# Batch 1 of a Fourier-mixing and GEGLU kernel loaded and folded like batch 0, with the weights ahead of it in the DMA queue

## The chip, the cores and the metric

One core of one Trainium2 chip. The metric is the device time of a run in microseconds (us); the time of before is the median of three runs. The core has a matrix engine (TensorE, PE), which takes a weight tile (LDWEIGHTS) and streams columns past it (MATMUL) into PSUM; a vector engine (VectorE, DVE); an activation engine (ScalarE, ACT); a general engine (GpSimd, POOL); and a sequencer (SyncE, SP) that here issues nearly all DMA transfers. Each engine works through its own instructions in the order in which the program gives them.

## The reference

`x` has 8 batches of 3008 tokens with 256 features. Each batch gets the real part of a two-dimensional Fourier transform (over tokens and features), and then every token goes through a gated feed-forward block with 1536 hidden units:

```python
X = np.fft.fft(x, axis=1)
X = np.fft.fft(X, axis=2)
x = X.real.astype(np.float32).reshape(B * S, D)

g = x @ w_gate
gelu = 0.5 * g * (1.0 + erf(g * inv_sqrt2))
val = x @ w_val
return (gelu * val @ w_out).astype(np.float32)
```

## The kernel before

**The transform.** 3008 = 64 x 47. A token index is split into 64 values on the partitions and 47 columns j. The kernel uses the symmetry of the real transform: feature f and feature 256 - f are added and subtracted first (the "folds"), so that 128 even and 128 odd values are left of 256. Stage one is a transform of length 64 along the partitions by tables of sines and cosines, stage two one of length 47 (`b_steps`, tables `TPQ`). Only 1505 of 3008 output rows are made (`Y`); the mirrored ones come from the even and odd parts of the layers that follow. The feature transform itself is folded into the weights: `gen_w` multiplies `w_gate` and `w_val` by a 256-point cosine table (`CW`) and leaves them as `WE`, `WOP`, `WOM`.

**Two ways through stage one.** Batch 0: `load_x` brings each third of the columns as three DMAs straight from `x`, with the partner columns (47 - j) on the odd partitions and the far columns in slots 4 to 7 of an `xin` buffer. `singles_first` and `fold_first` make 24 columns of folded data in `xf`, and `a_group` multiplies them by the table `G` (24 columns of 128). Batches 1 to 7: the tokens that are needed in mirrored order of the 64 are first copied, turned, from HBM to HBM (`flip`, two DMAs per batch, tile `xr`), and `load_x` takes four DMAs per third, two from `x` and two from `xr`. Then both folds are done (`fold_part`, two column pairs at a time, even step k = 0 and 2, odd step k = 1 and 3), which leaves 12 columns, and `a_step` multiplies each by a 128 x 128 table `GA` (made from `G` by `gen_ga`), two columns of 256 per step. Its result goes to HBM (`z_write`, tile `z`) and comes back with other partitions (`z_read`, into `Ap`) for stage two. POOL does the folds, but for batch 1 the step (1, 0) of `DVE_FOLDS` is DVE's.

**The layers.** The work is cut into units: batch, one of three chunks of rows, one of 12 tiles of 128 hidden units; 36 units a batch, 288 in all, numbered u, with i = u mod 36. In each unit PE does layer one (matmuls of up to 512 columns for gate and value, even, odd plus, odd minus), ACT the Gelu, DVE and POOL the products into `h`, and PE some matmuls of layer two of the chunk before (`Wo_sb`, 256 columns each) by the counts in `STEPS`. In the units of `SPLIT` the minus gate isn't a matmul of its own but is put together by ACT, DVE and POOL (`ge`, `go`).

**The order** is written out by hand. Ahead of the units stand batch 0's transform and the loads of the weights, in pieces of 256, 256, 512 and 512 columns; POOL casts them to bf16 (`cast_w`), and `gen_w` runs ahead of the units and in units 0 to 7 (`extra`): the last 512 columns in units 4 to 7. `f_units`, `a_units` and `r_units` say in which units the folds, `a_step`s and `z_read`s of the next batches stand; `plan` gives the units of stage two (from 22 on in batch 0). Layer two begins at the end of unit 12.

```python
    for f0, n in ((256, 256), (512, 512)):
        for i in (1, 0):
            load_w(f0, i, n)
    flip(1)
    pool.memset(xins[0][:, 4, :], 0.0)
    for i in (1, 0):
        load_w(1024, i)
    for i in range(3):
        load_x(1, i)
```

Of the kernel before, what the change touches and what calls it, by code (L numbers as in the profile page):

```python
# [10 lines left out]
BF16 = mybir.dt.bfloat16  # L11
INT32 = mybir.dt.int32
AF = mybir.ActivationFunctionType
ALU = mybir.AluOpType
# [24 lines left out]
def kernel(  # L39
# [24 lines left out]
    B, T, C = x.shape  # L64
# [2 lines left out]
    NJ = 48  # L67
    HJ = 24
    HP = HJ // 2
    DVE_FOLDS = ((1, 0),)  # L70
    KP = 96
    NG = 32
    NCH = C // 128
# [8 lines left out]
    psum = ctx.enter_context(tc.tile_pool(name="psum", bufs=1, space=bass.MemoryType.PSUM))  # L82
    dram = ctx.enter_context(tc.tile_pool(name="dram", bufs=1, space=bass.MemoryType.DRAM))

    G = const_pool.tile([128, HJ, 128], BF16)
    GA = const_pool.tile([128, HP, 128], BF16)
    GH = NG // 2
    TS = 2 * N2
# [120 lines left out]

    xr = {}  # L210

    def flip(b):
        xr[b] = xr_tile()
        for s, (j0, n) in enumerate(((N2 - HP + 1, HP - 1), (HP, HP))):
            d = xr[b][s, :, :, :]
            sync.dma_start(
                out=ap_replace(d, ap=[[C, n], [HP * C, N1], [1, C]], offset=d.offset),
                in_=ap_replace(x, ap=[[C, n], [-N2 * C, N1], [1, C]],
                               offset=x.offset + (b * T + N2 * (N1 - 1) + j0) * C))
# [25 lines left out]
    def singles_first(i):  # L245
        pool.tensor_tensor(
            _sub(xf, [[HP * C, 2], [C, 4], [128, 2]], 4 * i * C),
            _sub(xins[i], [[4 * C, 2], [C, 4], [128, 2]], 0),
            _sub(sg, [[0, 2], [0, 4], [1, 2]], 0), op=ALU.mult)

    def fold_first(i, a0, an):
        at = lambda o, k: _sub(xins[i], [[4 * C, 2], [C, an], [k, 127]], a0 * C + o)
        to = lambda o: _sub(xf, [[HP * C, 2], [C, an], [1, 127]], (4 * i + a0) * C + o)
        vec.tensor_tensor(to(1), at(1, 1), at(255, -1), op=ALU.add)
        for h in range(2):
            lo, hi = (_sub(xins[i], [[C, an], [k, 127]], (4 * h + a0) * C + o) for o, k in ((1, 1), (255, -1)))
            vec.tensor_tensor(
                _sub(xf, [[C, an], [1, 127]], (HP * h + 4 * i + a0) * C + 129),
                hi if h else lo, lo if h else hi, op=ALU.subtract)

    def fold_part(b, i, k):
        eng = vec if b == 1 and (i, k) in DVE_FOLDS else pool
        a0 = k // 2 * 2
        o0 = (HP * (b % 2) + 4 * i + a0) * C
        at = lambda s, o, pat: _sub(xins[i], [[C, 2]] + pat, (s + a0) * C + o)
        if k % 2 == 0:
            eng.tensor_tensor(
                _sub(xf, [[C, 2], [128, 2]], o0), at(0, 0, [[128, 2]]), at(4, 0, [[128, 2]]), op=ALU.add)
            eng.tensor_tensor(
                at(0, 1, [[128, 2], [1, 127]]), at(0, 1, [[128, 2], [1, 127]]),  # L270
                at(4, 255, [[-128, 2], [-1, 127]]), op=ALU.add)
        else:
            for o, op in ((1, ALU.add), (129, ALU.subtract)):
                eng.tensor_tensor(
                    _sub(xf, [[C, 2], [1, 127]], o0 + o), at(0, 1, [[1, 127]]),
                    at(0, 255, [[-1, 127]]), op=op)

# [121 lines left out]

    def sin_g(i):  # L400
        for h in range(2):
            act.activation(
                _sub(G, [[128, 8], [1, 64]], i * 8 * 128 + h * 64),
                _sub(reds[i], [[64, 8], [1, 64]], 0), AF.Sin, scale=col_h[h][:, :], bias=col_o[h][:, :])

    def turn_g(odd):
        nb = 2 if odd else 1
        for to, of, n, sign in (((1, 33, 8, 1.0), (33, 1, 8, -1.0), (3, 35, 8, -1.0), (35, 3, 8, 1.0))
                                if odd else ((0, 0, 16, 1.0), (2, 2, 16, -1.0))):
            pat = [[128, 8], [64, nb], [4, n]]  # L410
            to, of = _sub(G, pat, 16 * 128 + to), _sub(G, pat, of)
            if odd:
                act.activation(to, of, AF.Copy, scale=sign)
            else:
                pool.tensor_scalar(to, of, sign, None, op0=ALU.mult)

    def gen_ga():
        for h in range(2):
            act.activation(
                _sub(GA, [[128, HP], [1, 64]], 64 * h), _sub(G, [[128, HP], [1, 64]], HP * h * 128),  # L420
                AF.Copy, scale=half[:, h : h + 1])

    def phase_t():
# [152 lines left out]
    def a_group(J, v):  # L576
# [5 lines left out]
        for gq in range(2):  # L582
            for e in range(2):
                for jl in range(4):
                    jj = HP * (jl % 2) + 4 * J + 2 * v + jl // 2
                    on_half(ps, pe.matmul(
                        _sub(ps, [[1, 128]], gq * C + e * 128, 32 * jl, 32),
                        _sub(G, [[32, 2], [2, 16]], (jj - 16 * (jj > 15 and gq == 0)) * 128 + 64 * e + gq),
                        _sub(xf, [[1, 128]], jj * C + 128 * e), start=True, stop=True))
        if J:  # L590
            for h in range(2):
# [85 lines left out]
    units = []  # L677
    NU = B * len(CH) * NFC
    PER = NU // B
    STEPS = ((7, 8, 9, 8, 8, 8, 8, 8, 8, 8, 8, 8, 8, 9, 7, 8, 8, 8, 8, 8, 8, 8, 8, 8, 8, 9, 7, 7, 7, 10, 7, 7, 10, 8, 8, 8), (7, 9, 8, 8, 9, 7, 8, 8, 8, 7, 8, 9, 8, 7, 9, 9, 7, 8, 7, 5, 6, 6, 7, 5, 8, 8, 8, 8, 8, 8, 8, 8, 8, 8, 8, 8))  # L680
# [232 lines left out]

    WF = (4, 5)

    def warm(n, w=None):
        ps = ps_d()
        for _ in range(n):
            pe.matmul(ps, G[:, 0, :] if w is None else w, _sub(G, [[1, 512]], 0),
                      start=True, stop=True)  # L920

    for i in (1, 0):
# [81 lines left out]
    for u in range(NU + 2):  # L1004
# [142 lines left out]
```

## Time and profile before

| | |
|---|---|
| median of 3 runs | 619.86 us (619.02 to 620.75) |
| the profiled execution | 617.99 us, of which the span from first to last instruction is 616.0 |
| PE busy | 593.5 us, 96% |
| DVE, POOL, ACT busy | 561.7, 488.0, 473.7 us |
| granted TensorE clock, mean | 0.997 |
| DMA | 79.50 MB, mean 129 GB/s |

A row of the profile names the engine, the operation, what it writes and reads (`xf<-xin`), shapes, a count, and in brackets the idle time before it and what ended that. All instructions pass through one helper, so that nearly every row has line 26 (L26) and rows are told apart by their tiles. `SPq` is SP issuing a DMA; PEld is a weight load. "issue" stands for a wait of which the profile shows no releaser. The duration of one matmul contains its way through the array: matmuls that follow one another start at shorter distances than that.

### The profile page before, as it was taken

The page shows a single profiled execution, that of the slowest core. Times are in us where ns is not written, and L with a number is a line of the kernel's source. Part 1 is how long each engine was busy: PE and PEld are TensorE (multiplying, and loading weights), DVE is VectorE, ACT ScalarE, POOL GpSimd, SP SyncE. Part 2 cuts the span into 40 slices and gives each one's busy share as a digit, 9 for nine tenths or more (in the row PEclk, how much of TensorE's full clock was granted, in tenths as well). Part 3 has the DMA queues.
Part 4 walks back from the last instruction along what each step waited for, and adds up shares of the span by engine and source line. Part 5 has one row for each costly group of instructions (what it writes and reads, how often), then busy time and mean ns, then how long its engine had stood idle before and what let it go on. Part 6 is the DMA issues. An engine that isn't in the chain of part 4 may idle for free.

```text
span 616.0 us, 12455 instructions
## 1 busy us (share of the span) xinstructions
PE 593.5 (96%) x4285; PEld 389.4 (63%) x4285; DVE 561.7 (91%) x693; ACT 473.7 (77%) x985; POOL 488.0 (79%) x444
## 2 busy tenths in 40 slices
PE   4979899999999999999999999999999999999997
PEld 2535566666666666666666666666666666666666
DVE  7848889999999999999999999999999999999992
ACT  7868687878788788877878778887788778777762
POOL 6448989898978889898987979888987855666552
PEclk9989999999999999999999999999999999999999
DMA  7797733554543643545435545437224321222123
GB/s 250 237 315 245 240 125 77 160 162 122 160 123 84 192 150 94 156 118 169 142 89 146 155 112 159 133 86 213 63 61 103 80 59 44 61 51 53 38 49 85
DMA packets 75377, 79.50 MB, mean 129 GB/s; under 512 B 9291, under 2 KB 69515, under 8 KB 74643
## 3 DMA queue, kind: packets, MB, share of 16 engines
q1 hardware_dynamic: 73603, 77.81, 43.7%
q0 software_dynamic: 1552, 0.79, 0.9%
q8 instruction: 33, 0.54, 0.4%
q14 instruction: 29, 0.24, 0.1%
q10 hardware_dynamic: 160, 0.13, 0.1%
HBM read 48.52 MB, written 40.72 MB: 145 GB/s over the span
## 4 chain that ended last, share of the span: by engine, by line
PE 84%; DMA 6%; DVE 3%; SPq 3%; POOL 2%; issue 1%; ACT 1%; ACTq 0%; DVEq 0%; POOLq 0%
PE ps_o L26 36%; PE ps_g L26 26%; PE ps_v L26 18%; PE ps_d L26 4%; SPq L26 3%; DMA xin<-xr 2%; DMA wst<-in_moe_w_gate_dram 1%; DMA xin<-in_x_dram 1%; DMA Ap<-z 1%; DVE h L26 1%; POOL h L26 1%; DVE dv L26 1%; DVE ev L26 1%; DVE xf L26 0%; POOL go L26 0%
## 5 line engine op out<-in xcount | busy, mean ns | idle before, releaser
L26 POOL TENSOR_TENSOR h<-glm,dv 128x1024 bf16<-128x1024 bf16 (+1 forms) x138 | 291.1, 2112 | 82.4 <-DVE dv L26 43.7
L26 PE MATMUL ps_o<-Wo_sb,h 128*128 128x256 bf16 x2124 | 283.7, 273 | 0.0
L26 PEld LDWEIGHTS <-h 128*128 128x128 bf16 x2208 | 212.2, 98 | 70.3 <-issue 0.2
L26 DVE SCALAR_TENSOR_TENSOR ev<-nq,WN,ps_v 128x512 f32<-128x512 bf16 (+1 forms) x276 | 201.6, 734 | 24.2 <-PE ps_v L26 13.8
L26 ACT ACTIVATE glp<-ps_g 128x512 bf16<-128x512 f32 (+1 forms) x288 | 170.1, 591 | 43.2 <-PE ps_g L26 31.7
L26 ACT ACTIVATE glm<-ps_g 128x512 bf16<-128x512 f32 (+1 forms) x245 | 144.7, 591 | 60.0 <-PE ps_g L26 47.4
L26 DVE TENSOR_TENSOR h<-glp,ps_v 128x1024 bf16<-128x1024 bf16 (+2 forms) x150 | 173.0, 1153 | 8.8 <-ACT glp L26 8.0
L26 DVE SCALAR_TENSOR_TENSOR dv<-ev,ps_v 128x1024 f32<-128x1024 f32 (+1 forms) x138 | 164.9, 1195 | 0.0
L26 PE MATMUL ps_v<-Y,WE 128*128 128x512 bf16 (+1 forms) x288 | 108.3, 376 | 0.0
L26 PE MATMUL ps_v<-Y,WOP 128*128 128x512 bf16 (+1 forms) x288 | 108.2, 376 | 0.1
L26 PE MATMUL ps_g<-Y,WOP 128*128 128x512 bf16 (+1 forms) x288 | 108.1, 375 | 0.0
L26 PE MATMUL ps_g<-Y,WE 128*128 128x512 bf16 (+1 forms) x288 | 108.0, 375 | 0.0
L26 PEld LDWEIGHTS <-WOP 128*128 128x128 bf16 x576 | 55.8, 97 | 60.4 <-issue 1.3
L26 PE MATMUL ps_g<-Y,WOM 128*128 128x512 bf16 (+1 forms) x245 | 92.3, 377 | 0.5 <-DVE WOM L26 0.5
L26 PEld LDWEIGHTS <-WE 128*128 128x128 bf16 x576 | 56.3, 98 | 31.0 <-issue 5.1
L26 POOL TENSOR_TENSOR xf<-xin 128x254 bf16<-128x254 f32 (+1 forms) x125 | 68.4, 564 | 4.2 <-PE ps_d L26 3.6
L26 ACT ACTIVATE osb<-ps_o 128x512 f32<-128x512 f32 x92 | 54.2, 589 | 15.4 <-PE ps_o L26 11.5
L26 POOL TENSOR_TENSOR go<-go,ge 128x480 f32<-128x480 f32 (+1 forms) x43 | 53.0, 1232 | 11.9 <-DVE go L26 11.9
L26 POOL TENSOR_TENSOR xin<-xin 128x508 f32<-128x508 f32 x41 | 51.8, 1264 | 0.0
L26 PE MATMUL ps_d<-tab,Ap 96*128 96x94 bf16 (+2 forms) x246 | 43.8, 204 | 3.1 <-issue 2.1
L26 ACT ACTIVATE Y<-ps_d 128x192 bf16<-128x192 f32 (+5 forms) x156 | 38.8, 381 | 0.3 <-PE ps_d L26 0.3
L26 PEld LDWEIGHTS <-Ap 96*128 96x128 bf16 (+1 forms) x289 | 24.6, 96 | 15.2 <-issue 2.6
(132 smaller groups left out, 325.6 us busy)
## 6 DMA issues: line engine op xcount, KB each, us to landing
out_dram<-osb SPq DMA_DIRECT2D x358, 64.0 KB
xin<-in_x_dram SPq DMA_DIRECT2D x47, 256.0 KB
xin<-xr SPq DMA_DIRECT2D x35, 256.0 KB
xr<-in_x_dram SPq DMA_DIRECT2D x7, 768.0 KB
z<-S SPq DMA_DIRECT2D x21, 256.0 KB
Ap<-z SPq DMA_DIRECT2D x21, 256.0 KB
xr<-in_x_dram SPq DMA_DIRECT2D x7, 704.0 KB
nq<-nrow SPq DMA_DIRECT2D x8, 376.2 KB
```

The lines of the kernel that those rows point to most:

```text
L26: return lambda *a, **k: self._tc.keep_in_program_order(call(*a, **k))
```

## The change

Batch 1 goes through `load_x` and the folds the way batch 0 does: three DMAs per third, straight from `x`, no `flip(1)`. `fold_one` does it in steps of two column pairs as `fold_part` did (even steps with `singles_first`, odd steps with two subtractions), and fills all 24 columns of `xf`. Its stage one has no `GA`: for each of 12 columns j, for even and odd features (e), two products are added in PSUM, of columns j and 12 + j with a table each. For that `G` is laid out anew: for each pair (j, j + 12) and e there are 64 columns of one table, 64 zeros and 64 columns of the other, 192 in all, so that a window of 128 at offset 0 or 64 is one table beside zeros. The zeros are a DVE memset; the second pair of Sin calls becomes four; `turn_g(False)` turns the odd tables as well as the even.

The last third of the weights is issued right behind the second. `load_wo` moves from ahead of the units to unit 4, `gen_ga` from unit 8 to 18, and the memset of slot 4 of `xin` 0 from ahead of the units to unit 10. DVE's fold is step (1, 1). The units of folds, `a_step`s and `z_read`s, `STEPS` and `SPLIT` are written anew.

```diff
-    DVE_FOLDS = ((1, 0),)
+    DVE_FOLDS = ((1, 1),)
...
-    G = const_pool.tile([128, HJ, 128], BF16)
+    GS = 192
+    G = const_pool.tile([128, HP, 2, GS], BF16)
...
+    goff = lambda jj, e: (jj % HP * 2 + e) * GS + jj // HP * 128
...
-        if b == 0:
+        if b < 2:
             put_x(i, 1, 4, 4, xb(N2 - HP - j, [[-C, 4]]))
             put_x(i, 1, 1 - o, 3 + o, xb(N2 - 1 + o - j, [[-C, 3 + o]]))
             put_x(i, 0, 0, 8, xb(j, [[HP * C, 2], [C, 4]]))
...
+    def fold_even(i, a0, an, eng):
         at = lambda o, k: _sub(xins[i], [[4 * C, 2], [C, an], [k, 127]], a0 * C + o)
+        eng.tensor_tensor(
+            _sub(xf, [[HP * C, 2], [C, an], [1, 127]], (4 * i + a0) * C + 1),
+            at(1, 1), at(255, -1), op=ALU.add)
+
+    def fold_odd(i, a0, an, eng):
         for h in range(2):
             lo, hi = (_sub(xins[i], [[C, an], [k, 127]], (4 * h + a0) * C + o) for o, k in ((1, 1), (255, -1)))
-            vec.tensor_tensor(
+            eng.tensor_tensor(
                 _sub(xf, [[C, an], [1, 127]], (HP * h + 4 * i + a0) * C + 129),
                 hi if h else lo, lo if h else hi, op=ALU.subtract)
...
+    def fold_one(i, k):
+        eng = vec if (i, k) in DVE_FOLDS else pool
+        if k % 2 == 0:
+            singles_first(i, k, 2)
+            fold_even(i, k, 2, eng)
+        else:
+            fold_odd(i, k - 1, 2, eng)
...
+    vec.memset(_sub(G, [[GS, 2 * HP], [1, 64]], 64), 0.0)
...
         for h in range(2):
-            act.activation(
-                _sub(G, [[128, 8], [1, 64]], i * 8 * 128 + h * 64),
-                _sub(reds[i], [[64, 8], [1, 64]], 0), AF.Sin, scale=col_h[h][:, :], bias=col_o[h][:, :])
+            for j0, n in ((8 * i, 8),) if i == 0 else ((8, 4), (12, 4)):
+                act.activation(
+                    _sub(G, [[2 * GS, n], [1, 64]], goff(j0, h)),
+                    _sub(reds[i], [[64, n], [1, 64]], 64 * (j0 - 8 * i)), AF.Sin,
+                    scale=col_h[h][:, :], bias=col_o[h][:, :])
...
-            pat = [[128, 8], [64, nb], [4, n]]
-            to, of = _sub(G, pat, 16 * 128 + to), _sub(G, pat, of)
+            pat = [[2 * GS, 8], [GS, 2], [4, n]]
+            to, of = _sub(G, pat, goff(16, 0) + to), _sub(G, pat, of)
...
+            j = 2 * k + i
+            if b == 1:
+                for e in range(2):
+                    for h in range(2):
+                        pe.matmul(
+                            ps[:, i * C + 128 * e : i * C + 128 * e + 128],
+                            _sub(G, [[1, 128]], goff(j, e) + 64 * h),
+                            _sub(xf, [[1, 128]], (HP * h + j) * C + 128 * e), start=(h == 0), stop=(h == 1))
+                continue
...
-    SPLIT = ((13, 25), (1, 5, 7, 11, 19, 25, 31), (1, 5, 7, 11, 25, 31), (5, 11))
+    SPLIT = ((31,), (1, 5, 7, 11, 19, 25, 31), (1, 5, 7, 11, 25, 31), (7,))
...
-    flip(1)
-    pool.memset(xins[0][:, 4, :], 0.0)
     for i in (1, 0):
         load_w(1024, i)
...
-    load_wo()
-    extra = {1: [lambda: cast_w(1024)], 0: [lambda: turn_g(False)], 8: [gen_ga], 17: [gen_tf]}
+    extra = {1: [lambda: cast_w(1024)], 0: [lambda: turn_g(False)], 4: [load_wo], 18: [gen_ga], 17: [gen_tf]}
...
-    a_units = ((9, 10, 11, 13, 14, 17), (1, 2, 5, 6, 8, 12))
-    r_units = ((14, 15, 19), (5, 13, 14))
-    f_units = ((1, 2, 4, 5, 6, 7, 8, 9, 10, 12, 13, 14), (15, 18, 21, 23, 25, 26, 29, 30, 31, 32, 33, 35), (3, 8, 12, 13, 20, 21, 23, 26, 27, 29, 33, 35))
+    a_units = ((8, 9, 10, 11, 12, 14), (0, 2, 6, 7, 9, 12))
+    r_units = ((13, 14, 16), (4, 13, 14))
+    f_units = ((1, 2, 3, 4, 5, 6, 7, 8, 9, 10, 11, 13), (17, 19, 21, 22, 24, 25, 26, 29, 30, 31, 33, 34), (4, 10, 11, 16, 18, 19, 22, 26, 27, 28, 32, 35))
...
+            if b == 0 and i == loads[0]:
+                pool.memset(xins[0][:, 4, :], 0.0)
...
-                    fold_part(1, *divmod(f_units[0].index(i), 4))
+                    fold_one(*divmod(f_units[0].index(i), 4))
```

More of the change, by code (lines that the diff above doesn't have):

```diff
@@ L243, in load_x, with singles_first, fold_first @@
         put_x(i, 1, 4, 4, xv(1, j, [[C, 4]]))
-    def singles_first(i):
+    def singles_first(i, a0=0, an=4):
         pool.tensor_tensor(
[L247 to L251, printed above, removed]
+            _sub(xf, [[HP * C, 2], [C, an], [128, 2]], (4 * i + a0) * C),
+            _sub(xins[i], [[4 * C, 2], [C, an], [128, 2]], a0 * C),
+            _sub(sg, [[0, 2], [0, an], [1, 2]], 0), op=ALU.mult)
+    def fold_even(i, a0, an, eng):
         at = lambda o, k: _sub(xins[i], [[4 * C, 2], [C, an], [k, 127]], a0 * C + o)
-        to = lambda o: _sub(xf, [[HP * C, 2], [C, an], [1, 127]], (4 * i + a0) * C + o)
-        vec.tensor_tensor(to(1), at(1, 1), at(255, -1), op=ALU.add)
+        eng.tensor_tensor(
+            _sub(xf, [[HP * C, 2], [C, an], [1, 127]], (4 * i + a0) * C + 1),
+            at(1, 1), at(255, -1), op=ALU.add)
+    def fold_odd(i, a0, an, eng):
         for h in range(2):
             lo, hi = (_sub(xins[i], [[C, an], [k, 127]], (4 * h + a0) * C + o) for o, k in ((1, 1), (255, -1)))
-            vec.tensor_tensor(
+            eng.tensor_tensor(
                 _sub(xf, [[C, an], [1, 127]], (HP * h + 4 * i + a0) * C + 129),
                 hi if h else lo, lo if h else hi, op=ALU.subtract)
+    def fold_first(i, a0, an):
+        fold_even(i, a0, an, vec)
+        fold_odd(i, a0, an, vec)
+    def fold_one(i, k):
[5 more added lines that the diff above has]
+            fold_odd(i, k - 1, 2, eng)
     def fold_part(b, i, k):
-        eng = vec if b == 1 and (i, k) in DVE_FOLDS else pool
         a0 = k // 2 * 2
@@ L266, in fold_part @@
         if k % 2 == 0:
-            eng.tensor_tensor(
+            pool.tensor_tensor(
                 _sub(xf, [[C, 2], [128, 2]], o0), at(0, 0, [[128, 2]]), at(4, 0, [[128, 2]]), op=ALU.add)
-            eng.tensor_tensor(
+            pool.tensor_tensor(
                 at(0, 1, [[128, 2], [1, 127]]), at(0, 1, [[128, 2], [1, 127]]),
@@ L273, in fold_part @@
             for o, op in ((1, ALU.add), (129, ALU.subtract)):
-                eng.tensor_tensor(
+                pool.tensor_tensor(
                     _sub(xf, [[C, 2], [1, 127]], o0 + o), at(0, 1, [[1, 127]]),
@@ L419, in gen_ga @@
             act.activation(
-                _sub(GA, [[128, HP], [1, 64]], 64 * h), _sub(G, [[128, HP], [1, 64]], HP * h * 128),
+                _sub(GA, [[128, HP], [1, 64]], 64 * h), _sub(G, [[2 * GS, HP], [1, 64]], 128 * h),
                 AF.Copy, scale=half[:, h : h + 1])
@@ L587, in a_group @@
                         _sub(ps, [[1, 128]], gq * C + e * 128, 32 * jl, 32),
-                        _sub(G, [[32, 2], [2, 16]], (jj - 16 * (jj > 15 and gq == 0)) * 128 + 64 * e + gq),
+                        _sub(G, [[32, 2], [2, 16]], goff(jj - 16 * (jj > 15 and gq == 0), e) + gq),
                         _sub(xf, [[1, 128]], jj * C + 128 * e), start=True, stop=True))
@@ L679 @@
     PER = NU // B
-    STEPS = ((7, 8, 9, 8, 8, 8, 8, 8, 8, 8, 8, 8, 8, 9, 7, 8, 8, 8, 8, 8, 8, 8, 8, 8, 8, 9, 7, 7, 7, 10, 7, 7, 10, 8, 8, 8), (7, 9, 8, 8, 9, 7, 8, 8, 8, 7, 8, 9, 8, 7, 9, 9, 7, 8, 7, 5, 6, 6, 7, 5, 8, 8, 8, 8, 8, 8, 8, 8, 8, 8, 8, 8))
-    SPLIT = ((13, 25), (1, 5, 7, 11, 19, 25, 31), (1, 5, 7, 11, 25, 31), (5, 11))
+    STEPS = ((7, 9, 8, 8, 8, 8, 8, 8, 8, 8, 8, 8, 8, 9, 7, 9, 7, 8, 8, 8, 8, 8, 8, 8, 8, 9, 7, 8, 8, 8, 8, 6, 10, 8, 8, 8), (7, 9, 8, 8, 9, 7, 8, 8, 8, 7, 8, 9, 7, 8, 9, 8, 7, 9, 7, 5, 6, 6, 7, 5, 8, 8, 8, 8, 8, 8, 9, 8, 7, 9, 8, 7))
+    SPLIT = ((31,), (1, 5, 7, 11, 19, 25, 31), (1, 5, 7, 11, 25, 31), (7,))
     for b in range(B):
@@ L914, with warm @@
     WF = (4, 5)
-    def warm(n, w=None):
+    def warm(n):
         ps = ps_d()
         for _ in range(n):
-            pe.matmul(ps, G[:, 0, :] if w is None else w, _sub(G, [[1, 512]], 0),
+            pe.matmul(ps, _sub(G, [[1, 128]], 0), _sub(G, [[1, 512]], 0),
                       start=True, stop=True)
```

1 line of the change is left out of this document (removed).

## The prediction

> **What bounds the kernel now.** I read the page first, then busy time by stretch, then who TensorE (PE) waited for, then the timeline at each wait.
>
> ```profile
> PE 593.5 (96%) x4285; PEld 389.4 (63%) x4285; DVE 561.7 (91%) x693; ACT 473.7 (77%) x985; POOL 488.0 (79%) x444
> ```
>
> ```profile
> 23.40:32.90 9.50, 9.34 (x46) 3.98 (x45) 7.81 (x19) 8.95 (x22) 4.62 (x6) 1.00 0.92 314
> 32.90:53.90 21.00, 15.57 (x110) 7.47 (x110) 11.49 (x21) 14.17 (x29) 13.95 (x19) 0.92 0.99 266
> 53.90:75.40 21.50, 19.38 (x128) 12.15 (x127) 20.25 (x24) 15.21 (x28) 19.15 (x25) 1.00 0.86 272
> 75.40:120.00 44.60, 44.60 (x330) 30.06 (x331) 39.71 (x47) 36.29 (x82) 40.40 (x38) 1.00 0.42 123
> 120.00:600.00 480.00, 478.94 (x3388) 317.50 (x3386) 460.26 (x525) 377.47 (x776) 392.59 (x313) 1.00 0.39 110
> ```
>
> Each row gives a stretch, its length, then PE, weight loads, DVE, ACT and POOL busy, the granted clock, the DMA share and GB/s. From 75.4 us on PE is never free (44.60 of 44.60, then 478.94 of 480), so there the time is PE's own work, and a microsecond that PE gains earlier reaches the end. What can be gained lies between 32.9 and 75.4, where PE is idle for 5.43 and 2.12 us. There the DMA engines are full (0.99 and 0.86). So the opening is a matter of the order in which bytes arrive.
>
> ```profile
> PE ps_o L26 <- POOL wb L26: 3.2, 1, 3.2
> PE ps_d L26 <- issue: 2.1, 1, 2.1
> PE ps_v L26 <- DVE h L26: 1.8, 1, 1.8
> PE ps_g L26 <- DVE WOM L26: 0.5, 1, 0.5
> ```
>
> These are all of PE's waits in the two stretches (us in total, times, longest), 7.6 us. I take them one by one.
>
> **Stall A, the last third of W.**
>
> ```profile
> 20.86 1.86 SPq L26 DMA_DIRECT2D xr<-in_x_dram  x2
> 22.76 5.20 SPq L26 DMA_DIRECT2D wst<-in_moe_w_val_dram  x1
> 27.85 1.04 POOL L26 CAST wb<-wst 128x1024 bf16<-128x1024 f32 x1 [0.25 <-DMA wst<-in_moe_w_gate_dram]
> 34.98 1.04 POOL L26 CAST wb<-wst 128x1024 bf16<-128x1024 f32 x1 [3.57 <-DMA wst<-in_moe_w_val_dram]
> 36.06 1.01 PE L26 MATMUL ps_o<-wb,CW 128*128 128x512 bf16 x2 [3.19 <-POOL wb L26]
> 37.27 0.61 PE L26 MATMUL ps_v<-Y,WOP 128*128 128x481 bf16 x1
> 37.67 0.61 PE L26 MATMUL ps_g<-Y,WOM 128*128 128x480 bf16 x1
> 35.00:40.00 5.00, 3.94 (x12) 1.52 (x12) 0.27 (x1) 1.77 (x4) 2.05 (x2) 0.66 1.23 286
> ```
>
> SP issues the two turned copies of batch 1 (`flip(1)`: by the code 12 + 11 rows of 64 KB, 1.5 MB) ahead of W's last columns. POOL casts the second third of W at 27.85, and the last third's first half only at 34.98. PE stands 3.19 us, and the clock after it is 0.66 in the 5 us window: 0.34 x 5 = 1.7 us more (the matmuls of 480 columns start 0.40 us apart). The change takes the 1.5 MB away, and W's last 1.05 MB come next. At the 314 GB/s of that stretch they are in 3.3 us after 27.85, so by 31.2.
>
> POOL gets there a little earlier than it must: `load_wo` no longer stands ahead, but `turn_g(False)` is doubled.
>
> ```profile
> 30.11 1.29 POOL L26 TENSOR_SCALAR G<-G 128x128 bf16<-128x128 bf16 x2
> 19.18 1.42 POOL L26 TENSOR_SCALAR tab<-red,cols 128x24 bf16<-128x24 f32 x4 [4.15 <-ACT red L26]
> 28.83 1.24 POOL L26 DMA_DIRECT2D Wo_sb<-in_moe_w_out_dram  x1
> ```
>
> One of 24 elements takes 0.36 us, one of 128 takes 0.65, so one of 256 some 1.0, and the pair 2.0. POOL: cast to 28.9, turn to 30.9, cast of the last third 30.9 to 32.0 and 32.0 to 33.0. PE wants the first at 36.06 - 3.19 = 32.87. The margin is 0.9 us. I count all of A as gained: -3.2 and -1.7.
>
> An idle 3.19 us brought the lower clock here; the idle 2.12 us of stall C, below, did not (1.00 in its stretch).
>
> **Stall B, a fold on DVE.**
>
> ```profile
> 45.87 0.18 DVE L26 TENSOR_TENSOR xf<-xin 128x4 bf16<-128x4 f32 x1 [3.00 <-DMA xin<-xr]
> 45.95 0.68 DVE L26 TENSOR_TENSOR xin<-xin 128x508 f32<-128x508 f32 x1
> 47.26 0.36 PE L26 MATMUL ps_v<-Y,WOM 128*128 128x480 bf16 x1 [1.81 <-DVE h L26]
> ```
>
> DVE serves in order and stands 3.00 us before its fold of batch 1, whose rows come back through the turned copy. The products behind it are late, and PE waits 1.81 and then 0.5. After the change DVE's fold is the odd half of the same third, still in unit 6, two instructions of 254 in place of 4 + 508, so the same work to 0.1 us. Its rows (by the code 1.05 MB per third, straight from x, behind W) land at about 34.2, 37.3 and 40.5 by the same 314 GB/s, a little less for what of the copy had already moved by 27.85. DVE came to this fold at 42.87 (45.87 - 3.00); without stall A's 4.9 us that is 38.0, and the second third is in at 37.3. I take -2.3, and +0.1 for what may stay of it (1 us if the rows come 1.7 later).
>
> **Stall C, the return of batch 1 from HBM.**
>
> ```profile
> 70.57 0.59 SPq L26 DMA_DIRECT2D Ap<-z  x1
> 75.39 0.21 PE L26 MATMUL ps_d<-tab,Ap 96*128 96x94 bf16 x2 [2.12 <-issue]
> ```
>
> PE stands 2.12 us until the last `z_read`, issued in unit 19 and 4.8 us on the way, is in. Now it is issued in unit 16, and stage one of the last two columns runs in unit 14, not 17. That is three units earlier for a reader that stays in unit 22, at about 2 us each (of 288 units some 22 lie ahead of 75.4, the other 266 fill 525 us). -2.1. Late next would be SP: it stops in unit 10 at `load_x(2, 0)` for the second turned copy, as before, and now also for POOL's memset, which is queued behind that unit's folds; behind SP stand the writes of z from unit 11 on. The slack of 6 us covers it; without it the 2.1 are back.
>
> Gains: 3.2 + 1.7 + 2.3 + 2.1 = 9.3 us.
>
> **What is added on PE.**
>
> ```profile
> 604.03 6.71 PE L26 MATMUL ps_g<-Wo_sb,h 128*128 128x256 bf16 x60
> 79.79 0.29 PE L26 MATMUL ps_d<-tab,Ap 96*128 96x94 bf16 x3
> 43.07 1.34 PE L26 MATMUL ps_d<-CW,wb 128*128 128x1 bf16 x48
> L26 PE MATMUL ps_d<-xf,GA 128*128 128x256 bf16 x84 | 16.0, 273 | 0.0
> L26 PE MATMUL ps_d<-tab,Ap 96*128 96x94 bf16 x228 | 43.4, 207 | 3.1 <-issue 2.1 <-DMA Ap<-z 1.0
> ```
>
> Stage one of batch 1 was 12 matmuls of 256 columns and becomes 48 of 128, each with a weight load. Sixty of 256 columns, each with its own weights, take (6.71 - 0.27) / 59 = 0.109 us each. Three of 94 columns take (0.29 - 0.21) / 2 = 0.04 each, so 128 columns 0.055 to 0.057. The 48 of one column, each with 128 columns of weights, take 0.028 each, so the load is not the limit. 48 x 0.057 - 12 x 0.109 = 2.7 - 1.3 = +1.4 us, all on PE.
>
> In the Trainium skill, "TensorE: Matmul & The Clock Gate", section "Back-to-back issue gap", pairs of weight load and matmul of 128 columns come every 81 ns. By it the term would be 48 x 0.081 - 1.3 = 2.6, and the sum 1.2 us more. This trace doesn't bear it out: the row of 94 columns has 0.04 a pair.
>
> Split units go from 2 to 1 in batch 0 and in batch 7: two more gate matmuls of up to 512 columns, 2 x 0.218 (0.218 is twice the 0.109) = +0.4 us on PE, for less on DVE, ACT and POOL, which the bound does not feel.
>
> **The front.**
>
> ```profile
> 0.85 0.27 DVE L26 MEMSET xin<- 128x256 f32 x1 [0.85 <-PEq L1131]
> 5.30 2.91 ACT L26 ACTIVATE G<-dv,col_o,col_h 128x512 bf16<-128x512 int32 x4
> 8.12 1.31 ACT L26 ACTIVATE G<-G 128x128 bf16<-128x128 bf16 x4
> 8.43 2.44 DVE L26 TENSOR_TENSOR xf<-xin 128x1016 bf16<-128x1016 f32 x3 [1.94 <-DMA xin<-in_x_dram]
> ```
>
> The memset of the zero columns is 24 x 64 = 1536 elements on DVE: 0.8 us by bytes of the 256-element row, 1.6 by elements. The second pair of Sin calls becomes four, half as long each, about +0.4 for the two more. The table G is then ready 1.2 to 2.0 us after 9.43 (8.12 + 1.31), at 10.6 to 11.4, if nothing of it is hidden. Stage one of batch 0 wants DVE's first folds too, which begin at 8.43 with the data and end at 10.87. So 0 to 0.6, and I take +0.1; without that cover it is the whole 1.2 to 2.0.
>
> **Wo, the new danger.**
>
> ```profile
> Wo_sb<-in_moe_w_out_dram POOLq DMA_DIRECT2D x1, 768.0 KB, 16.5
> 53.89 0.60 PE L26 MATMUL ps_o<-Wo_sb,h 128*128 128x256 bf16 x4
> L26 POOL TENSOR_TENSOR xin<-xin 128x508 f32<-128x508 f32 x41 | 51.8, 1264 | 0.0
> L26 POOL TENSOR_TENSOR xf<-xin 128x254 bf16<-128x254 f32 x84 | 59.5, 731 | 0.6
> ```
>
> Wo was issued at 28.83, landed 16.5 us later at 45.3, and is first read at 53.89, in unit 12. Now POOL issues it after three folds of batch 1. POOL's folds cost as before (1.26 and some 0.2 for the single columns an even step, 2 x 0.73 an odd one), and the first waits for its rows at 34.2: 35.6, 37.0, 38.4. So Wo is issued near 38.4 (37.5 if the rows come faster). PE reaches unit 12's layer two earlier than before by 3.2 + 1.7 + 2.3 less 0.1, and later by 1.6, since five steps of stage one lie ahead of it (5 x 8 x 0.057, as above) where three did (3 x 2 x 0.109); so at 48.4. Bounds of the landing: 16.5 us after issue again is 54.9; the bytes alone at 314 GB/s give 41. In between, the engines then have the rest of batch 1 (to 40.5), then 0.4 MB of the nq row spread over 128 partitions, 1.5 MB of turned copy, 0.5 MB of batch 2 and Wo's 0.8 MB: 3.2 MB at 272 GB/s end at 52.2 if all end together, and Wo, which shares them, ends ahead of the last, near 50.2. That case is the nearest to the traffic of that time, and I take it: PE stands 1.8 us. Bounds 0 and 6.5 + 1.7 of clock.
>
> **The sum.** -9.3 + 0.1 (B's rest) + 1.4 + 0.4 + 0.1 + 1.8 = -5.5 us. The profiled execution took 617.99 us (span 616.0), so 612.5; the median of the runs is 619.86, 1.9 above it, so I forecast 614.4. The rest of the change (new units for folds, reads and steps of later batches, steps of layer two with the same sums of 288 and 276 a batch, `gen_ga` in unit 18) falls where PE idles 1.06 us in 480: nothing, unless a step comes late.
>
> **The rivals.**
> 1. Wo is in time. The DMA engines idle for a moment while SP waits for the nq row to land, and Wo's bytes use it. Then the 1.8 fall away: 612.6, 612.3 if DVE's fold, the front and the narrow matmuls cost at their low ends, and 611.2 with a microsecond of what the runs of before differ (619.02 to 620.75). For it: Wo alone needs 3 us. Chance 0.25.
> 2. Wo is later, and the change loses: issued at 39.5, a microsecond later than forecast, with 16.5 us on the way as measured, it lands at 56.0. PE stands 7.6 us, and after more than 3.19 us idle the half clock costs 1.7. -7.3 + 9.3 = +2.0: 621.9. A landing after 55.9 makes the change slower, one between 52.1 (3.7 us idle and the clock) and 55.9 no change. For it: 16.5 us is what was measured. Against it: then the end of W, the copy and batch 1 were in front of it. Chance 0.19, of which 0.09 beyond +0.3%.
> 3. The copy is not what kept W back: the last third still lands near 35, A stays, and the narrow matmuls and Wo eat B and C: 618 to 620. Against it: the engines are full to 1.23 in that very window. Chance 0.08.
> 4. Weight loads and short matmuls don't overlap: 0.028 + 0.055 a pair, 48 x 0.083 - 1.3 = 2.7 in place of 1.4: 615.7. Chance 0.05, since pairs of 256 columns run at 0.109, about twice what 128 would take. This is what the 81 ns of the Trainium skill, quoted above, would give.
>
> **How the numbers follow.** The forecast has chance 0.43 and a range of its own of 613.4 to 616.5. A measurement tells 0.3% (1.9 us) from no change. Faster than 618.0: 0.43 + 0.25 + 0.05 + 0.03 of 3, 0.76; within: 0.10 of 2 and 0.05 of 3, 0.15; slower than 621.7: 0.09. The range 611.2 to 619.6 takes in rival 1 to its low end and rival 3, and leaves out 0.15 above (most of 2) and some 0.05 below.
>
> **What would show it.** In the profile after: no wait of PE on `wb` and clock 1.00 from 25 to 45 us (A); DVE's wait for its fold under 0.5 us (B); no wait of PE before the first Ap of batch 1 (C); matmuls of 128 columns on ps_d 0.057 us apart; PE's first read of Wo_sb near 50 us, and a wait before it of about 2 us; PE without gaps from unit 22 on, so that its unit 22 starts about 5 us earlier. I am wrong if PE waits on Wo_sb for 5 us or more, if POOL's folds make stage one late in units 8 to 14, or if gaps appear after 75 us.

## The result, and the profile after

Four executions of the changed kernel took 619.67, 618.87, 609.35 and 609.91 us, beside 619.02 to 620.75 us of before (median 620.28 of four). Its time over that of before is 0.9831 [0.9803, 0.986], about 609.8 us; this ratio is of the two shorter executions, since the comparison leaves out what lies over 1.5% above the fastest. The profile that came with the result is of the 619.67 us execution (span 617.8). The unedited kernel was therefore run again (first experiment) and gave 609.77 to 611.5 and a profile of 609.77 us (span 607.9). So there are two profiles of one program, "long" and "short" below, and comparing them shows more than either against before.

Busy time by stretch, columns as in the prediction; first the short execution, then the long one:

```profile
23.40:32.90 9.50, 9.37 (x47) 4.16 (x46) 7.65 (x18) 9.13 (x22) 6.66 (x8) 1.00 1.04 369
32.90:53.90 21.00, 19.17 (x179) 11.67 (x178) 17.84 (x25) 16.49 (x33) 17.21 (x26) 1.00 0.91 246
53.90:75.40 21.50, 20.82 (x145) 12.98 (x143) 19.49 (x22) 17.22 (x36) 17.68 (x21) 1.00 0.67 205
75.40:120.00 44.60, 44.60 (x327) 30.40 (x325) 42.47 (x51) 36.90 (x78) 41.10 (x36) 1.00 0.44 125
```

```profile
32.90:53.90 21.00, 11.94 (x101) 6.57 (x100) 18.50 (x16) 9.29 (x19) 15.49 (x23) 0.76 0.79 203
53.90:75.40 21.50, 20.82 (x154) 13.29 (x153) 17.25 (x23) 17.01 (x30) 9.63 (x16) 1.00 0.69 205
```

In the short execution PE is busy 19.17 of 21.00 where it was 15.57 before, at clock 1.00 and no longer 0.92. In the long one it is busy 11.94, at clock 0.76. After 53.9 the two agree (20.82 both). What separates them happens between 32.9 and 53.9, but for 0.8 us ahead of unit 0, which starts at 22.84 in the short and at 23.60 in the long one.

PE's waits, all of the short execution's and then the longest of the long one's (total, times, longest; the waits on `prow`, `S` and `xf` lie in batch 0's transform, ahead of 19 us, in both):

```profile
PE ps_o L26 <- POOL prow L26: 6.5, 7, 4.3
PE ps_v L26 <- DVE h L26: 1.8, 1, 1.8
PE ps_v L26 <- POOL xf L26: 1.2, 1, 1.2
PE ps_d L26 <- ACT S L26: 0.8, 1, 0.8
PE ps_g L26 <- ACT glp L26: 0.7, 1, 0.7
PE ps_v L26 <- DVE xf L26: 0.5, 2, 0.3
```

```profile
PE ps_v L26 <- DVE h L26: 9.1, 1, 9.1
```

The waits on `wb` (stall A) and on the last `z_read` (stall C) are gone from both. There is no wait on `Wo_sb` in either. The wait on DVE's `h`, stall B, has stayed: 1.8 us in one and 9.1 in the other. DVE's rows show what DVE does in that time, in the short and then in the long execution (start, duration; the bracket would give idle time before the row, and there is none). The fold is two instructions: one row holds both in the short execution, and the row of the long one is the second alone (the first took 0.98).

```profile
37.30 3.78 DVE L26 TENSOR_TENSOR xf<-xin 128x254 bf16<-128x254 f32 x2
41.01 0.65 DVE L26 TENSOR_TENSOR h<-glp,ps_v 128x481 bf16<-128x481 bf16 x1
```

```profile
38.97 10.13 DVE L26 TENSOR_TENSOR xf<-xin 128x254 bf16<-128x254 f32 x1
49.02 0.65 DVE L26 TENSOR_TENSOR h<-glp,ps_v 128x481 bf16<-128x481 bf16 x1
```

The fold no longer waits for rows. It runs, and is slow. In the long execution one instruction of 254 elements takes 10.13 us; before, one of 508 elements took 0.68. POOL's rows of the long execution beside it:

```profile
37.92 1.26 POOL L26 DMA_DIRECT2D Wo_sb<-in_moe_w_out_dram  x1
39.20 1.32 POOL L26 TENSOR_TENSOR xf<-xin 128x254 bf16<-128x254 f32 x2
...
40.64 1.25 POOL L26 TENSOR_TENSOR xf<-xin 128x508 bf16<-128x508 f32 x1
...
45.86 0.30 POOL L26 MEMSET xin<- 128x256 f32 x1
...
47.56 1.25 POOL L26 TENSOR_TENSOR xf<-xin 128x508 bf16<-128x508 f32 x1
49.73 0.61 POOL L26 COPY hx<-h 128x512 bf16<-128x512 bf16 x1 [0.92 <-DVE h L26]
```

POOL folds without a break from 39.20 to 48.81 (a memset of 0.30 us among the folds), and DVE's instruction, begun at 38.97, ends at 49.10, as POOL runs out of work. The rows that DVE needs were in: POOL's even step of the same two column pairs, the fold of 40.64, read them without a wait, 7 us before DVE was done. Before, POOL's folds of batch 1 follow one another nearly as closely, after one wait ahead of the first of them:

```profile
41.71 0.22 POOL L26 TENSOR_TENSOR xf<-xin 128x4 bf16<-128x4 f32 x1 [3.58 <-PE ps_d L26]
...
44.74 1.25 POOL L26 TENSOR_TENSOR xin<-xin 128x508 f32<-128x508 f32 x1
46.07 3.37 POOL L26 TENSOR_TENSOR xf<-xin 128x254 bf16<-128x254 f32 x5
```

There DVE, kept until 45.87 by its rows, came to the end of one of POOL's folds (45.99) and got through at once; POOL's next fold took 1.15 us where those behind it took 0.72. Whether the gap of 0.08 us between these two folds, which the folds of the change don't have, let it through isn't shown.

### The profile page after: what moved, and what is told of

Read it like the earlier page. It is cut to its first block, busy times and chain, and to the rows that moved or that the text cites. A ratio compares the mean times of both kernels' runs of the same rounds, so it can differ in the third digit from the quotient of the medians.

```text
span 617.8 us, 12524 instructions
## 1 busy us (share of the span) xinstructions
PE 594.0 (96%) x4323; PEld 391.8 (63%) x4323; DVE 572.3 (93%) x692; ACT 473.6 (77%) x985; POOL 486.0 (79%) x442
## 4 chain that ended last, share of the span: by engine, by line
PE 92%; DVE 4%; ACT 1%; DMA 1%; issue 0%; DVEq 0%
PE ps_o L26 38%; PE ps_g L26 29%; PE ps_v L26 20%; PE ps_d L26 6%; DVE xf L26 2%; DVE h L26 1%; DMA xin<-in_x_dram 1%; ACT glm L26 0%; ACT glp L26 0%; DVE ev L26 0%; DVE dv L26 0%; ACT GA L26 0%; DVE WOM L26 0%; ACT S L26 0%; DVE G L26 0%
## 5 line engine op out<-in xcount | busy, mean ns | idle before, releaser
L26 POOL TENSOR_TENSOR xf<-xin 128x254 bf16<-128x254 f32 (+2 forms) x124 | 72.7, 601 | 0.0
L26 POOL TENSOR_TENSOR go<-go,ge 128x480 f32<-128x480 f32 (+1 forms) x41 | 50.5, 1231 | 5.8 <-DVE go L26 5.8
L26 POOL TENSOR_TENSOR xin<-xin 128x508 f32<-128x508 f32 x36 | 45.5, 1264 | 0.0
L26 ACT ACTIVATE S<-ps_d 128x512 bf16<-128x512 f32 (+1 forms) x43 | 25.2, 586 | 10.4 <-PE ps_d L26 10.4
```

Source lines behind the costliest of these rows:

```text
L26: return lambda *a, **k: self._tc.keep_in_program_order(call(*a, **k))
```

## The experiments: what holds DVE's fold

The theory: DVE's fold, which reads two operands from SBUF, is held up while POOL folds without a pause; how long depends on whether it meets POOL's break at `load_wo`. The rivals: the rows of that third are late after all; or Wo's transfer and its place are what makes the long executions. All ratios below are over runs of before beside them, with a 95% interval.

**The change again, unedited.**

> The changed kernel once more, unedited. In its first profile DVE's second fold of batch 1 (128x254) took 10.13 us where 0.4 is usual, POOL was folding without a pause at that time, and PE stood 9.06 us. Theory: where DVE gets through, the fold takes 0.4 us, the kernel takes 608 to 611 us, PE has no wait over 2 us after unit 4, and what it gains over the kernel before is the stalls A, B and C (9 us) less 2 us of matmuls and about 1 us before Wo. Rival: the 10 us are always there and hide gains elsewhere: 618 to 620 in all executions.

610.52 us (609.77 to 611.5, four runs), 0.9848 [0.9828, 0.9869]. Its profile is the short one above. With the first four, 2 executions of 8 were long. The profiles don't bear out the theory's part on `load_wo`. In the short execution the fold begins in that break of POOL (37.30; the break lasts from 36.43 to 37.69), but its two instructions end behind it, at 39.53 and 41.09, between folds of POOL. In the long one the first ends in the break (39.04; the break ends at 39.18), and the second is the one held for 10.13 us.

**All folds on POOL.**

```diff
-    DVE_FOLDS = ((1, 1),)
+    DVE_FOLDS = ()
```

> The changed kernel with all folds of batch 1 on POOL, none on DVE. Theory (DVE's fold reads two operands from the same memory as POOL's folds and is held off while POOL reads without a pause): no DVE instruction over 1.5 us between 30 and 60 us, PE's 9 us wait is gone in every execution; POOL is 1.3 us later with what follows, so 609 to 612 us. Rival (the long DVE instruction has to do with the stretch, with DMA or with the clock, and not with the two engines): another DVE instruction between 35 and 50 us takes several us, and about half of the executions stay at 618 to 620.

611.65 us (609.57 to 615.16), 0.9881 [0.985, 0.9912]. The wait on `h` is gone, and the next one shows:

```profile
PE ps_o L26 <- DMA Wo_sb<-in_moe_w_out_dram: 1.0, 1, 1.0
```

So B's wait was DVE's fold, but it was hiding one on Wo: without it PE comes to layer two before Wo (issued at 37.41, 12.2 us on the way) is in. Two of six runs took 615 us; neither of these was profiled, and their cause is open.

**Wo ahead of the units again.** POOL's break of 1.26 us at `load_wo` moves away from the fold; Wo itself comes earlier.

```diff
+    load_wo()
-    extra = {..., 4: [load_wo], 18: [gen_ga], ...}
+    extra = {..., 18: [gen_ga], ...}
```

> The changed kernel with load_wo back ahead of the units, as in the kernel before. Theory by the forecast's term (PE stands 1.8 us for Wo in unit 12): 1 to 2 us faster than the changed kernel, as long as W's last third and batch 1 still come in time, though Wo's 0.8 MB then delay them by some 2 us. Rival (Wo is in time in unit 4 as well, and early it only takes bytes from batch 1): 0 to 3 us slower. In its profile the wait of PE on the third of W or on DVE's fold shows which.

617.95 us (609.35 to 620.24, twelve runs, ten of them above 615), 0.9943 [0.9914, 0.9971]. Neither expected range held (1 to 2 us faster, 0 to 3 slower): an earlier Wo made the kernel 7.4 us slower than the change, so Wo's transfer isn't what the long executions wait for. The profile has the fold and the wait:

```profile
37.24 9.06 DVE L26 TENSOR_TENSOR xf<-xin 128x254 bf16<-128x254 f32 x1
```

```profile
PE ps_v L26 <- DVE h L26: 7.4, 1, 7.4
```

Here the first of the two instructions is held. It ends at 46.30, 0.28 us after the last of POOL's train (46.02), and the second, beside an idle POOL, takes 0.41.

**The same with a pause for DVE.** Two POOL memsets of 512 elements into tiles that nothing reads then, in unit 6, where DVE's fold stands. POOL has more work, not less.

```diff
+    def pause():
+        for t in (go_tile(), ge_tile()):
+            pool.memset(t, 0.0)
...
+    load_wo()
+    extra = {..., 6: [pause], 18: [gen_ga], ...}
```

> load_wo ahead of the units, where DVE's fold of batch 1 took 9.4 us for the pair and PE stood 7.4 us, and at the end of unit 6, on POOL, two memsets of 512 elements (about 1.2 us, they write and read nothing). Theory (DVE's instruction with two operands from SBUF is held off by POOL instructions that read SBUF, and gets through when POOL stops reading): DVE's fold ends within 0.6 us of the first memset's start, PE's wait on DVE's products is under 3 us, 609 to 614 us. Rival (any work of POOL without a pause holds it off, or it is not POOL at all): the fold still takes 7 us or more, 616 to 619.

609.24 us (609.05 to 609.41, four runs), 0.9831 [0.9801, 0.9861]: two added instructions take 8.7 us off the kernel above, and none of its runs is long. DVE's row, and POOL's memset:

```profile
37.58 2.82 DVE L26 TENSOR_TENSOR xf<-xin 128x254 bf16<-128x254 f32 x2
```

```profile
38.86 1.25 POOL L26 TENSOR_TENSOR xf<-xin 128x508 bf16<-128x508 f32 x1
40.06 0.51 POOL L26 MEMSET go<- 128x512 f32 x1
```

The fold ends at 40.40, 0.34 us after the memset began and while POOL is busy with it. Rows that came late would not come for a memset: the first rival falls here too. But this is the second instruction; the first had ended at 38.25, between two folds of POOL, with no memset near.

**The same with copies in place of memsets.** If any pause in the folds would do, an instruction that reads SBUF serves as well.

```diff
-            pool.memset(t, 0.0)
+            pool.tensor_copy(t, _sub(xins[1], [[1, 512]], 0))
```

> The same with two copies of 512 elements from an xin buffer in place of the two memsets: POOL works about as long at the same place, but reads SBUF. Theory: DVE's fold is held off as without them, 7 us or more, PE waits 6 us or more, 616 to 619 us in most executions. Rival (the change of POOL's instruction or the shift of its later folds lets DVE through): as with the memsets, 609 to 614.

609.34, 620.14, 619.7 and 619.32 us. The profile fell on the first, in which the fold ended at 40.45, 0.33 us after the first copy began at 40.12, just as with the memset. By their times three of four were long with copies, which read, and none of four with memsets. That speaks for POOL's reads as what DVE competes with; so does the first copy, which took 0.80 us where the second took 0.60, while both memsets took 0.51. With four runs of each, and no profile of a long one with copies, it isn't settled, nor is what let DVE through beside a copy once.

## The experiments: the parts of the change by themselves

**Before again**, one execution: 617.74 us, with stalls A, B and C as before (2.0 on `wb`, 2.3 on `h`, 1.8 at C). It isn't longer than the first profile's 617.99, so it can't tell where the longer runs of before lose their time. It corrects a reading of the prediction, however: there 3.19 us of standing brought the lower clock and 2.12 did not; here A's 2.04 us, which ended at 35.03, did (0.56 from 36 to 38, the row below), and B's 2.35 too (0.62 from 46 to 48). So the length of the standing alone doesn't decide it.

> The kernel before once more, unedited, for a second profile. Its timed runs lie 1 to 2 us above its first profile (617.99). Theory: PE's three stalls A, B and C are there again with their causes, and one of them is longer than in the first profile by as much as the run is. Rival: the same stalls, and the difference lies evenly over the span.

```profile
36.00:38.00 2.00, 2.00 (x8) 0.75 (x6) 0.45 (x1) 1.40 (x3) 0.92 (x1) 0.56 1.25 274
```

**W first, alone.** In the kernel before, only the order of the copy and the last third of W is changed.

```diff
-    flip(1)
-    pool.memset(xins[0][:, 4, :], 0.0)
     for i in (1, 0):
         load_w(1024, i)
+    flip(1)
+    pool.memset(xins[0][:, 4, :], 0.0)
```

> The kernel before with flip(1) and the memset behind W's last third: part one of the change alone. Theory (the 1.5 MB of copies kept W back): PE's wait on the last third of W and the half clock go, 4.9 us, but the copy and with it batch 1 come 3 us later, so that the waits of DVE's fold and of stage two grow by up to that: 614 to 619. Rival (W's third comes no earlier): 619 to 621, with PE's wait on wb still 3 us.

620.42 us, 1.0 [0.998, 1.0019]. It was expected at 614 to 619. Stall A is gone, and unit 8 starts 5.3 us earlier (0.3 of it is there at unit 4). Then the copy is late, and everything is given back at B and C:

```profile
PE ps_v L26 <- DVE h L26: 7.1, 1, 7.1
...
PE ps_d L26 <- issue: 3.3, 1, 3.3
```

```profile
45.84 0.26 DVE L26 TENSOR_TENSOR xf<-xin 128x4 bf16<-128x4 f32 x1 [8.16 <-DMA xin<-xr]
```

Here DVE is idle 8.16 us for rows: the same wait of PE as in the long execution of the change, with another cause, which only DVE's row tells apart.

**Before, with all folds on POOL.**

```diff
-    DVE_FOLDS = ((1, 0),)
+    DVE_FOLDS = ()
```

> The kernel before with all folds of batch 1 on POOL. It tests stall B alone: theory, the waits of PE of 1.8 and 0.5 us near 47 us go, since DVE no longer stands before the rows of batch 1, and POOL's 1.4 us more delay stage one of batch 1 a little: 1 to 2.3 us faster than the kernel before, 617.5 to 619. Rival (PE meets the same wait a little later at stage one, because the rows of batch 1 are late anyway): within 0.5 us of the kernel before.

621.63 us, 1.0024 [1.0004, 1.0044]. B's wait is gone and unit 12 starts 2.0 us earlier, though 0.75 of that is there at unit 8 already; stall C grows from 2.1 to 5.8. My expectation that B's gain would stay was wrong: ahead of a stall in the same chain a gain only moves the wait.

**The change with all folds on POOL and Wo in unit 2.** Both waits that the first group found are taken away together.

```diff
-    DVE_FOLDS = ((1, 1),)
+    DVE_FOLDS = ()
...
-    extra = {..., 4: [load_wo], 18: [gen_ga], ...}
+    extra = {..., 2: [load_wo], 18: [gen_ga], ...}
```

> The changed kernel with all folds of batch 1 on POOL and load_wo in unit 2. Theory: with no fold on DVE PE has no wait on DVE's products near unit 8, and Wo issued two units and one fold earlier lands 1.4 us or more earlier, so that the wait of 1.0 us on Wo goes too: 607.5 to 609.5, about 1 us under the clean runs of the changed kernel, and no execution over 612. Rival (POOL, now with all folds, is the bound of the opening): the wait only moves to the folds of unit 12, and the time is that of the kernel with all folds on POOL, 609.5 to 612.

608.9 us (608.54 to 609.25, six runs), 0.9813 [0.9789, 0.9837]: faster than before. All six lie under the change's shortest run (609.35), though the intervals of the two ratios overlap, and they differ by 0.7 us where the change's differ by 10. Neither the wait on `h` nor one on `Wo_sb` is left. The next three are edits of this kernel.

**With the later batches' schedule of before** (`f_units[1:]`, `a_units[1]`, `r_units[1]` and `STEPS` as they were).

```diff
-    a_units = ((8, 9, 10, 11, 12, 14), (0, 2, 6, 7, 9, 12))
-    r_units = ((13, 14, 16), (4, 13, 14))
+    a_units = ((8, 9, 10, 11, 12, 14), (1, 2, 5, 6, 8, 12))
+    r_units = ((13, 14, 16), (5, 13, 14))
...
```

> The same, with the units of folds, stage one and reads of batches 2 to 7 and the steps of layer two as in the kernel before. Theory from the unit starts of the profiles: from unit 36 to the end the changed kernel gains 1.7 us more, 1.0 of it at one wait for the return of a batch from HBM near unit 165: 1 to 2 us slower than the same kernel with the new units, and that wait is back. Rival (the 1.7 us come from the two split units fewer or from PE's lead): within 0.5 us.

610.31 us (610.15 to 610.86), 0.9836 [0.9812, 0.986]. The new schedule of the later batches is worth 1.4 us; no run of the one reaches into the other's range. But the wait that I expected back, of PE on `Ap<-z`, isn't in the profile. PE waits on ACT's `glm` instead, once, at 105.8 us in batch 1:

```profile
PE ps_g L26 <- ACT glm L26: 1.2, 1, 1.2
```

**With the split units of before.**

```diff
-    SPLIT = ((31,), ..., (7,))
+    SPLIT = ((13, 25), ..., (5, 11))
```

> All folds on POOL and load_wo in unit 2, with the split units of the kernel before (13 and 25 in batch 0, 5 and 11 in batch 7). Forecast's term: two gate matmuls fewer, 0.4 us faster. Rival (ACT, DVE and POOL pay for a split unit in the opening, where they have no more to give): 0 to 1 us slower.

610.64 us (610.06 to 612.34), 0.9859 [0.9835, 0.9882], 1.7 us more than without. The profile says where: three waits of stage one on POOL's folds.

```profile
PE ps_d L26 <- POOL xf L26: 2.5, 3, 1.7
```

**Batch 1's stage one as 12 matmuls of 256 columns.** One matmul for each column, without the second product and the odd features' own table, so that the sums are incomplete; this prices the 48 narrow ones.

```diff
-                for e in range(2):
-                    for h in range(2):
-                        pe.matmul(
...
+                pe.matmul(
+                    ps[:, i * C : (i + 1) * C], _sub(G, [[1, 128]], goff(j, 0)),
+                    _sub(xf, [[1, C]], j * C), start=True, stop=True)
```

> All folds on POOL and load_wo in unit 2, with stage one of batch 1 as 12 matmuls of 256 columns: the second product of each pair and the odd table are left out. The forecast's term for the 36 matmuls more is 1.4 us of PE. Theory: PE is the bound in units 8 to 14 only in part (ACT and DVE take as long), so 0.3 to 1.4 us faster than the same kernel with 48. Rival: nothing, under 0.3, since POOL's folds set those units.

609.92 us (607.72 to 611.23), 0.9835 [0.9809, 0.986]: no gain, though unit 17 starts 0.9 us earlier (55.97 for 56.84; 0.13 of it is there at unit 8, ahead of the edit). Later, in the profiled execution, the longest of the six (611.23), PE waits on DMAs that the other kernel doesn't wait for:

```profile
PE ps_d L26 <- DMA out_dram<-osb: 2.1, 3, 0.9
...
PE ps_d L26 <- DMA Ap<-z: 0.7, 1, 0.7
```

So 0.7 us of the 1.4 is seen at unit 17, and the time of the whole doesn't settle the rest. Whether the waits come from the edit is open.

## Why the prediction was right or wrong

The direction was right; the gain was put at 5.5 us and was 8.2 between the profiles (617.99 to 609.77), and the time, 609.8 by the ratio, lay below the range I gave (611.2 to 619.6). Several terms failed, and not all in one direction. Below the range it came by Wo (a wait of 1.8 us forecast, none measured), by the rest of the change (nothing forecast, -1.7), by the front (+0.1 forecast, -0.6) and by the base (1.1 too high), 5.3 us together; the fold on DVE (2.2 us of gain forecast, 0.5 measured) and a new wait of 0.7 took some 2.4 of that back. That the forecast was no further off is the luck of errors that cancel. I take the terms in the order of the sum. Where a unit starts is read from its first matmul `ps_v<-Y,WE`:

| first matmul of unit | before | change, short | difference |
|---|---|---|---|
| 4 | 31.44 | 30.74 | -0.70 |
| 8 | 44.27 | 38.71 | -5.56 |
| 12 | 52.75 | 47.54 | -5.21 |
| 22 | 72.13 | 67.99 | -4.15 |
| 23 | 76.57 | 70.11 | -6.46 |
| 148 | 325.28 | 318.25 | -7.04 |
| 172 | 373.08 | 365.03 | -8.05 |
| 287 | 599.01 | 590.81 | -8.19 |

**A, right.** Between units 4 and 8 the change gains 4.9 us, and 3.2 + 1.7 were forecast. POOL's steps went as worked out, in the short execution:

```profile
27.94 2.28 POOL L26 TENSOR_SCALAR G<-G 128x256 bf16<-128x256 bf16 x2
30.03 2.03 POOL L26 CAST wb<-wst 128x1024 bf16<-128x1024 f32 x2
```

The turn of both tables took 2.28 for the 2.0 forecast, and the last cast ends at 32.1 (forecast 33.0).

**C, right.** Between units 22 and 23: 2.3 gained, 2.1 forecast.

**B, the step that failed first.** I wrote that DVE's fold is "the same work to 0.1 us" and took -2.3 for its rows being in. They were in, and the fold took 3.78 or over 10 us: I priced the instruction by its elements, from a row in which DVE got through at once (POOL's fold of 44.74 took 1.25, the next began at 46.07, and DVE's at 45.95). Of B only the 0.5 us on `WOM` were gained in the short execution. The same work was now held beside POOL's folds, and I had not asked what DVE's instruction shares with them. My sign for B, a wait of DVE for its fold under 0.5 us, came true and showed nothing: DVE didn't wait, its instruction was slow. The Trainium skill, "SBUF — State Buffer", section "Who interferes with whom", says that a DVE instruction with two SBUF inputs contends with a GpSimd instruction that reads SBUF, not with one that only writes it, and calls the contention an exclusive lock. The runs speak for this sort of instruction (with memsets of 0.51 us none of four runs was long, with copies three of four), and the block here lasted through a train of fifteen instructions, 10.13 us.

**Wo, the wrong one of two cases.** I put PE's wait at 1.8; it was 0. Wo was issued at 36.43 and 11.2 us on the way, so it landed at 47.6, and PE's first read stands at 49.11 (forecast: landing 50.2, PE at 48.4). That is the outcome of rival 1:

```profile
32.41 0.23 POOL L26 TENSOR_TENSOR xf<-xin,sg 128x8 bf16<-128x8 f32 x1 [0.35 <-PE ps_v L26]
36.43 1.26 POOL L26 DMA_DIRECT2D Wo_sb<-in_moe_w_out_dram  x1
Wo_sb<-in_moe_w_out_dram POOLq DMA_DIRECT2D x1, 768.0 KB, 11.2
49.11 0.93 PE L26 MATMUL ps_o<-Wo_sb,h 128*128 128x256 bf16 x7
```

The term that failed is the landing, and in it the issue above all. POOL's first fold began at 32.41 and not at 34.2, so Wo was issued 2.0 us earlier than the 38.4 forecast; on the way it was 11.2, hardly less than the 11.8 forecast. The DMA engines did idle as rival 1 has it (a share of 0.22 from 36 to 38 us), but that made Wo's way little shorter. PE's side moved too: its first read came 0.7 later than forecast. The danger was near, however: with B's wait gone PE waited 1.0 us on Wo. The dangers I named in the opposite direction, rivals 2 and 3, are excluded for this order by the absence of any wait on `Wo_sb` and of one on `wb`.

**The narrow matmuls, right in their spacing; rival 4 wrong.**

```profile
43.76 0.61 PE L26 MATMUL ps_d<-xf,G 128*128 128x128 bf16 x8
L26 PE MATMUL ps_d<-xf,G 128*128 128x128 bf16 x48 | 3.7, 219 | 0.0
```

Eight in 0.61, one alone takes 0.22, so (0.61 - 0.22) / 7 = 0.056 us apart; 0.057 was forecast, and 48 x 0.056 - 1.3 = 1.4 on PE, of which the run without 36 of them shows 0.7 at unit 17. By the 81 ns of the Trainium skill, "TensorE: Matmul & The Clock Gate", section "Back-to-back issue gap", the eight would have taken an estimated 0.79; they took 0.61.

**The split units, wrong sign.** I counted two more matmuls on PE, +0.4, and called the work saved on DVE, ACT and POOL nothing because the bound doesn't feel it. In the opening, with POOL folding without a pause, it does: the old split cost 1.7 us in the kernel where it was tried, with 2.5 us of PE's waits on POOL's folds. The +0.4 by itself no run shows.

**"The rest of the change", wrong at zero.** Undone, the later batches' schedule cost 1.4 us. Between the profiles -6.46 at unit 23 grows to -8.19 at unit 287, and 1.0 of that falls between units 148 and 172, where a wait on `Ap<-z` of 1.0 us that before has isn't there now. I had that wait in the profile ("PE idles 1.06 us in 480") and dismissed it. But with the old schedule back it isn't this wait that returns, and the second profile of before has only 0.4 us on `Ap<-z`. So the size of the term is shown, and what in the schedule makes it is open. The one new wait, 0.7 on `glp`, went uncosted.

**The front, and the base.** I allowed +0.1 ahead of unit 0; this execution starts it 0.56 earlier, and other executions of the change up to 0.2 later, so that is scatter. And I set the forecast 1.9 us above the sum, for the runs of before lie that far above its profiled execution. The changed kernel's median, 610.52, lies only 0.75 above its own profile, so 1.1 of the error is not the mechanism's at all. The stalls of before differ between its two profiles (A 3.2 and 2.0), and its runs may scatter with them.

Taken together, in the short execution: A -4.9, the rest of B -0.5, C -2.3, matmuls +1.4, `glp` +0.7, front -0.6, later batches -1.7: -7.9 of the 8.2 measured. The split units' +0.4 isn't in this sum. Of what would show me wrong I had named POOL's folds, but making stage one late, not holding DVE.

## What to carry to other kernels

When a change moves an instruction, ask what the other engines do beside its new place: here a DVE instruction with two operands in SBUF had to be priced by POOL's folds next to it, not by its elements alone. A wait named by the profile says who was late, not why; look whether the late engine's row is a long idle time before a short instruction or a long instruction. And parts that give nothing alone (W first: 1.0; POOL's folds before the change: 1.0024) can pay as parts of a whole, since each alone only moves the wait to the next stall of the chain.

## What the hardware showed that I had not expected

One DVE subtraction of 254 elements per partition stood for 10.13 us beside a train of POOL folds and ended 0.29 us after the train did (48.81 to 49.10). POOL's folds were not slowed in it (1.25 us for 508 elements); in the short execution, where DVE got through, POOL's neighbouring fold took 1.49 instead. Over the profiles this has a form: each of the eight fold instructions of DVE that ran beside POOL's folds ended 0.26 to 0.30 us after the end of one of POOL's instructions (39.53 after 39.23 and 41.09 after 40.83 in the short execution), and where POOL's next one followed at once and reads SBUF, it took 0.17 to 0.24 us longer than its like elsewhere. So, by these rows, DVE gets its turn at a boundary, and at most boundaries it doesn't. A memset of 0.30 us in the train (45.86) didn't free it; beside one of 0.51 it got through, after 0.34. One program so has two durations 9 us apart; what decides between them isn't shown. PE's clock in and after the stall (0.50 from 45 to 50 us, 0.60 from 50 to 55) is part of the price:

```profile
45.00:50.00 5.00, 0.28 (x1) 0.10 (x1) 5.00 (x3) 0.00 (x0) 4.08 (x7) 0.50 1.05 206
50.00:55.00 5.00, 5.00 (x28) 3.00 (x27) 3.23 (x6) 2.44 (x5) 0.34 (x1) 0.60 0.18 25
```

Why DVE passes at some boundaries between POOL's instructions and not at others stays open.
